# Query-key-normalised attention: streamed share for the zero matmuls, doubled instead of tripled score waves, sums of squares on TensorE, norm steps on GpSimd

## The chip, the cores and the metric

One Trainium2 chip, one of its cores. The metric is the device time of one execution in microseconds (us). Before the change it is 632.83 us, the median of three runs (632.67 to 633.11). The profiled execution is a run of its own: 633.45 us, of which the instructions span 631.5 us.

## What is computed

32 heads, 2048 queries and keys, 20 numbers per head:

```
qn = q / (sqrt((q * q).sum(-1, keepdims=True)) + 1e-6)
kn = k / (sqrt((k * k).sum(-1, keepdims=True)) + 1e-6)
logits = einsum('bhqd,bhkd->bhqk', qn, kn) * t[None, :, None, None]
out = einsum('bhqk,bhkd->bhqd', softmax(logits), v)      # B=1 H=32 S=2048 Dh=20
```

The inputs are bf16, and so is the output.

## The kernel before

**Tiles.** Four heads form a head group (`hg`, 8 of them), 512 queries a query group (4 per head group). A *tile* is 128 keys of one head against 512 queries; there are 32 x 16 x 4 = 2048. One head group and one query group make a *sub-block* (`sb`): 64 tiles, whose results add up in one PSUM bank, `psO`. There are 32 sub-blocks, and at the end of each `psO` is drained by a VectorE transpose into `accT` (L360), while TensorE may not write it.

**Two ways to exponentials.** TensorE writes a tile's scores into PSUM (L692: the four heads sit in four 32-row strips of the array, and strips run side by side). Then either ScalarE takes `exp` of two tiles at once, `psA` to `pA` (L885; here called a *wave*; `psA` holds two waves, so the scores of wave w wait until the `exp` of wave w-2 has ended), or VectorE turns a tile in `psD` into the bits of an f16 with one multiply-add to int16 (`dI`, "P1", L325), of which two shifted copies `dS` are made by adding integers: on VectorE (L340) or on GpSimd (L338). Then TensorE multiplies with `vaug` (V and a column of ones, for the denominators), L714: one matmul for a ScalarE tile, four for a VectorE tile (`dI` with `vaug` and with `vhalf`, and each `dS` with `vaug`), in four 32-column strips side by side.

**Zeros.** A matmul of zeros adds nothing to `psO` and keeps TensorE streaming (L558, 128 columns each; at the start 11 of 512 columns, L562). While `psO` drains there can be none; there the score matmuls of a wave are issued three times over (`mms * 3`), to the same place with the same result.

**Preparation.** For each head group k, q and v are loaded (L395, L405), squared (`sq`, L260) and reduced (L263) on VectorE, turned into reciprocal norms by eight small steps on VectorE (`rs0` to `rs5`, `eps`, `inv`, L282 to L289), multiplied into `kpad` and `qpad` (L304, GpSimd), and transposed by DMA into `kT` and `qT` (L414). The first head group goes in two parts: rows 0 to 3 by TensorE, and of rows 4 to 15 the `kT` rows 8 to 15 and the `qT` rows 4 to 15 by DMA.

**What sets the order.** No scheduler on the chip: `make_plan` walks a model of the core in steps of 5 ns, with costs in constants, and writes down one order for each engine; the chip then runs these orders with semaphore waits. So each engine and the DMA queue of SyncE issue strictly in order: an instruction that waits holds all behind it. The constants decide the order, not the duration of anything. `in_use` says how busy TensorE was in a window `HEATW`, and zeros are put in below `HEAT`. VectorE and GpSimd share a port: `lock` keeps VectorE's fast modes off it while GpSimd runs. Two plans are built, and a branch early in the program takes the first if no `t` is above a bound, as here.

Of the kernel before, what the change touches and what calls it, by code (L numbers as in the profile page):

```python
# [6 lines left out]
BF16 = mybir.dt.bfloat16  # L7
# [20 lines left out]
NH = 4  # L28
WAVES = (2, 2)
DBANKS = 3  # L30
NPA = 20
RING = 24
RUN_MAX = 4
# [3 lines left out]
D_LAST = 18  # L37
D_WAIT = 36
# [3 lines left out]
PREP1 = (.25,.35)  # L42
# [3 lines left out]
HOLD = 0  # L46
# [7 lines left out]
POOL_MAX = 3  # L54
ALONE = (.2, 0)
PMIN = 5
PGAP = 0.3
PVHOLD = (.22,.22)
HEAT0 = 11
HEATN = 128  # L60
HEAT = .57
HEATW = 3.41
# [3 lines left out]
ACT0 = .05  # L66
ACT1 = .24
# [10 lines left out]
PSLACK = 0.15  # L78
# [3 lines left out]
SOON = 8  # L82
DURG = 1
LOAD1 = 0.2
DJOIN = 0.3
# [60 lines left out]
def bass_standalone__qk_norm__prompt_kernel(  # L146
# [15 lines left out]
    with ExitStack() as es:  # L162
# [16 lines left out]
        vaug = [sbuf(f"vaug{i}", [128, NH, R, 32], BF16) for i in range(2)]  # L179
        vpart = {c: [sbuf(f"v{n}{i}", [128, NH, R, 32], BF16) for i in range(2)] for c, n in ((.5, "half"),)}  # L180
# [7 lines left out]
        idn = sbuf("idn", [128, 128], BF16)  # L188
        nr0 = sbuf("nr0", [128, 2, NH, 4], F32)
# [41 lines left out]
        def prep_ops(hg, r0, r1, a0=0, a1=2, pool=False):  # L231
# [9 lines left out]
            for c0 in range(r0, r1, sqn * 2 // na):  # L241
# [30 lines left out]
            def add(nm, emit, reads, writes, rate=R1, fix=0.0):  # L272
                ops.append(dve(nm, n, rate, emit, reads, writes, fix))
# [5 lines left out]
            else:  # L279

                y = ri.bitcast(F32)
                add("rs0", lambda e: e.tensor_scalar(ri, s_.bitcast(I32), -0.5, RS_MAGIC, ALU.mult, ALU.add), [SS], [K("ri")], R2)  # L282
                add("rs1", lambda e: e.tensor_tensor(rb, s_, y, ALU.mult), [K("ri"), SS], [K("rb")])
# [58 lines left out]
        def part_op(hg, c):  # L342
            b = hg % 2
            f = lambda tl: tl[b][:, :, :, :].rearrange("p h r d -> p (h r d)")
            return dve("vh", NH * R * 32, R4, lambda e: e.tensor_single_scalar(f(vpart[c]), f(vaug), c, ALU.mult),
# [34 lines left out]
        def load_qk(hg, a, part=None):  # L380
            b = hg % 2
            r0, r1 = (0, R) if part is None else PARTS[part]
            if a == 0 and hg == HG - 1:

                ops = []
                for x in range(4):
# [10 lines left out]
                        0.5, 4.0 if part != 0 else 2.2)]  # L397
# [10 lines left out]
        def tr_op(hg, which, r0, r1):  # L408
# [6 lines left out]
                       [(which + "pad", b, r) for r in range(r0, r1)], keys, 0.58 + 0.17 * (r1 - r0), 1.75 + 0.17 * (r1 - r0))  # L415
# [21 lines left out]
        def make_plan(share):  # L437
# [61 lines left out]
            def zeros(i, after=()):  # L499
                z = lambda ap_, val, key: Op("POOL", "z", lambda e: e.memset(ap_, val), after, [(key, i)], 0.5, 0.6)  # L500
                return [z(kpad[i][:, :, :, D:32], 0.0, "kz"), z(qpad[i][:, :, :, D:32], 0.0, "qz"),
                        z(vaug[i][:, :, :, D:D + 1], 1.0, "vz"), z(vaug[i][:, :, :, D + 1:32], 0.0, "vz")]
# [3 lines left out]
                               [], ["iot"], 0.5, 0.6)] + zeros(0))  # L506
# [54 lines left out]
            o = Op("PE", "heat", None, ["zt"], [("psA", 0)])  # L561
            o.info = [(lambda e, i=i: e.matmul(psA[:, (i % 3) * QW:(i % 3 + 1) * QW], zt[:, 0:128], zt[:, :])) for i in range(HEAT0)]  # L562
# [3 lines left out]
            used_w = [(0.0, 0.0, 0.0)]  # L566
# [52 lines left out]
            if share:  # L619
                for c in vpart:  # L620
                    o = part_op(0, c)
                    o.reads.append(("qpad", 0, R - 1))
                    want_dve(o, 3)
            loaded = 1
# [42 lines left out]
            def pe_put(op, mode, strips):  # L667
# [11 lines left out]
                if st - used_w[0][0] > 20:  # L679
                    del used_w[0:20]  # L680
# [651 lines left out]
```

## Time and profile before

| | |
|---|---|
| median of 3 runs | 632.83 us |
| profiled execution, its span | 633.45 us, 631.5 us |
| busy: TensorE, VectorE, ScalarE, GpSimd | 614.5, 614.1, 618.8, 445.5 us |
| `exp` instructions on ScalarE | 667 (1333 tiles) |
| tiles on VectorE | 715 |
| TensorE clock granted, mean | 0.995 |

In a line of the profile stand the source line, the engine, the operation, what is written and read, the shapes and the count; then busy time and the mean duration of one, then the idle time just before and what ended it. In a timeline the first number is the start and the second the length of a run of like instructions, in us. Consecutive instructions of an engine overlap a little in the records, so the step from one to the next is shorter than the duration of one.

### The profile page before, as it was taken

The numbers are of one execution on the slowest core, as the hardware profiler recorded it, in microseconds if no ns is written. First come the engines' busy times: TensorE is split into PE (matmuls) and PEld (weight loads), VectorE is DVE, ScalarE is ACT, GpSimd is POOL, SyncE is SP. The second block draws the span as 40 slices with busy tenths as digits, with TensorE's granted clock in tenths as the row PEclk, the third lists the DMA queues.
The fourth block names the chain that finished last, engine by engine and source line by source line (L and its number), as shares of the span: only waits on it lengthen the run. The fifth ranks groups of instructions, "written<-read, shape, count | busy, mean of one in ns | idle before, by whom it ended". The sixth has DMA issues, their size and how long they took to land.

```text
span 631.5 us, 15864 instructions
## 1 busy us (share of the span) xinstructions
PE 614.5 (97%) x6794; PEld 180.3 (29%) x6794; DVE 614.1 (97%) x869; ACT 618.8 (98%) x675; POOL 445.5 (71%) x491
## 2 busy tenths in 40 slices
PE   8999999999999999999999999999999999999996
PEld 4432222322222232223223222232222332222221
DVE  6999999999999999999999999999999999999995
ACT  6999999999999999999999999999999999999995
POOL 4586667766677776876768666776777777666772
PEclk8999999999999999999999999999999999999999
DMA  6610404041040130306031050400404022010000
GB/s 73 88 10 16 95 1 43 2 62 48 2 43 2 35 76 5 39 2 111 1 29 16 1 110 3 40 4 3 93 3 57 2 33 37 1 23 6 6 5 13
DMA packets 113772, 19.57 MB, mean 31 GB/s; under 512 B 102944, under 2 KB 113696, under 8 KB 113696
## 3 DMA queue, kind: packets, MB, share of 16 engines
q1 hardware_dynamic: 112896, 18.37, 19.9%
q8 instruction: 55, 0.90, 0.6%
q10 hardware_dynamic: 800, 0.12, 0.1%
q14 instruction: 21, 0.17, 0.1%
HBM read 7.87 MB, written 2.62 MB: 17 GB/s over the span
## 4 chain that ended last, share of the span: by engine, by line
ACT 72%; PE 26%; DVE 1%; DMA 0%; issue 0%; POOL 0%
ACT pA L885 72%; PE psO L714 12%; PE psA L692 10%; PE psD L692 2%; PE psO L558 2%; DMA qk<-in_q_dram 0%; DVE ssum L263 0%; POOL kpad L304 0%; DVE accT L360 0%; PE psD L570 0%; DVE sqs L260 0%; DVE ost L368 0%; DVE qT L585 0%; DVE rn L289 0%; DVE rec L364 0%
## 5 line engine op out<-in xcount | busy, mean ns | idle before, releaser
L885 ACT ACTIVATE pA<-psA 128x1024 f16<-128x1024 f32 (+1 forms) x667 | 614.5, 1111 | 2.0 <-PE psA L692 1.6
L338 POOL TENSOR_TENSOR dS<-dI,shc 128x256 int32<-128x256 int32 (+2 forms) x378 | 373.0, 1007 | 130.0 <-DVE dS L340 93.2
L325 DVE TENSOR_SCALAR dI<-psD 128x1024 int16<-128x1024 f32 (+1 forms) x486 | 434.1, 927 | 4.4 <-PE psD L692 1.8
L692 PE MATMUL psA<-qT,kT 32*128 32x512 bf16 x1553 | 283.0, 384 | 8.9 <-ACT pA L885 6.0
L714 PE MATMUL psO<-pA,vaug 128*32 128x512 f16 (+1 forms) x1333 | 233.7, 384 | 0.0
L714 PE MATMUL psO<-dS,vaug 128*32 128x512 f16 x1430 | 224.5, 385 | 0.0
L692 PE MATMUL psD<-qT,kT 32*128 32x512 bf16 x715 | 193.9, 383 | 0.0
L714 PE MATMUL psO<-dI,vaug 128*32 128x512 f16 x715 | 155.3, 386 | 0.0
L714 PE MATMUL psO<-dI,vhalf 128*32 128x512 f16 x715 | 152.0, 384 | 0.0
L692 PEld LDWEIGHTS psA<-qT,kT 32*128 32x128 bf16 x1553 | 69.0, 91 | 239.4 <-ACT pA L885 224.1
L340 DVE TENSOR_SCALAR dS<-dI 128x2048 int16<-128x2048 int16 (+2 forms) x182 | 122.5, 679 | 0.0
L714 PEld LDWEIGHTS psO<-dS,vaug 128*32 128x32 bf16 x1430 | 51.1, 94 | 73.2 <-issue 58.7
L714 PEld LDWEIGHTS psO<-pA,vaug 128*32 128x32 bf16 x1333 | 52.5, 94 | 37.5 <-issue 31.8
L692 PEld LDWEIGHTS psD<-qT,kT 32*128 32x128 bf16 x715 | 45.4, 91 | 22.1 <-DVE dI L325 10.2
L714 PEld LDWEIGHTS psO<-dI,vaug 128*32 128x32 bf16 x715 | 36.7, 93 | 24.5 <-issue 17.4
L714 PEld LDWEIGHTS psO<-dI,vhalf 128*32 128x32 bf16 x715 | 36.4, 94 | 22.0 <-issue 19.2
L366 POOL TENSOR_TENSOR ost<-accT,rec 128x320 bf16<-128x320 f32 x31 | 23.3, 753 | 16.7 <-DVE dS L340 9.5
L304 POOL TENSOR_TENSOR qpad<-qk,rn 128x320 bf16<-128x320 bf16 x31 | 22.0, 728 | 17.3 <-DVE dS L340 10.4
L558 PE MATMUL psO<-zt 128*128 128x128 bf16 x310 | 32.3, 228 | 0.1
L304 POOL TENSOR_TENSOR kpad<-qk,rn 128x320 bf16<-128x320 bf16 x31 | 22.2, 738 | 10.8 <-DVE dS L340 6.1
L558 PEld LDWEIGHTS psO<-zt 128*128 128x128 bf16 x310 | 19.7, 101 | 21.0 <-issue 20.1
L360 DVE STREAM_TRANSPOSE accT<-psO 128x512 f32<-128x512 f32 x32 | 22.6, 705 | 2.7 <-PE psO L714 2.7
(51 smaller groups left out, 100.1 us busy)
## 6 DMA issues: line engine op xcount, KB each, us to landing
vaug<-in_v_dram SPq DMA_DIRECT2D x32, 80.0 KB, 4.0
qk<-in_k_dram SPq DMA_DIRECT2D x7, 320.0 KB, 4.0
out_dram<-ost SPq DMA_DIRECT2D x28, 80.0 KB, 1.9
qk<-in_q_dram SPq DMA_DIRECT2D x6, 320.0 KB, 3.9
qk<-in_q_dram SPq DMA_DIRECT2D x4, 80.0 KB, 3.1
out_dram<-ost SPq DMA_DIRECT2D x7, 40.0 KB, 2.0
qk<-in_k_dram SPq DMA_DIRECT2D x1, 240.0 KB, 3.6
qk<-in_q_dram SPq DMA_DIRECT2D x1, 240.0 KB, 4.2
```

What stands on the lines that cost most here:

```text
L304: emit = lambda e, o=dst, x=src, s=sc: e.tensor_tensor(o, x, s, ALU.mult)
L325: lambda e: e.tensor_scalar(dst, psD[:, pb * QW:(pb + n) * QW], 1024.0 * LOG2E, 15360.0 - 1024.0 * LOG2K + SHIFTS[0], ALU.mult, ALU.add),
L338: lambda e: e.tensor_tensor(o.bitcast(I32), x.bitcast(I32), c, ALU.add), rd + ["shc"], wr)
L340: lambda e: e.tensor_single_scalar(o, x, float(SHIFTS[i] - SHIFTS[0]), ALU.add), rd, wr)
L360: dve("drain", QW, R1, lambda e: e.transpose(aT[:, :, :].rearrange("p b d -> p (b d)"), psO[:, :]), ["psO"], [("accT", b)], 0.03),
L366: pool_op("omul", 320, True, lambda e: e.tensor_tensor(dst, num, rcb, ALU.mult), [("accT", b), ("rec", b)], [("ost", ob, qg)]) if pool else
L558: return lambda e: e.matmul(bank, zt[:, 0:128], zt[:, 0:n], start=False, stop=False, skip_group_check=True)
L692: return lambda e: e.matmul(dst, lhsT, rhs, tile_position=(32 * hh, 0))
L714: return lambda e: e.matmul(dst, lhsT, rhs, start=first, stop=last, skip_group_check=True, tile_position=(0, 32 * hh))
L885: a = Op("ACT", "exp", lambda e, s=src, d=dst: e.activation(d, s, ACT.Exp), [("psA", slot)], [("pA", pslot, i) for i in range(WAVES[slot]) ...
```

## The change

- The planner's measure for zeros becomes the share of the last 1.7 us in which anything streamed through TensorE (before: 3.41 us, weighted by the share of strips in use).
- While `psO` drains, a wave's scores are issued twice, not three times, and below a share of 0.8.
- For head groups 1 to 7 the squares (still VectorE) are transposed by DMA (`sqT`) and summed by TensorE against a matrix of ones and zeros (`ind`): 20 matmuls of 128 columns, in five lots of four, into a `psD` bank lent for it. `rs0` and `rs1` read the sums there. `ind` is made at the start (GpSimd and VectorE).
- `rs2`, `rs3`, `rs4` and `eps` of these groups go to GpSimd.
- `vaug` and `vhalf` have 22 columns per head, not 32.
- The planner's constants change: 18 wave slots in `pA` instead of 20, at most 30 shifts waiting instead of 36, shifts of up to 6 tiles at once on VectorE and of at most 2 on GpSimd (before 4 and 3), other lead times, other latencies for loads and transposes. `LOAD1 = 0` (before 0.2): the loads of head group 1 are asked for as soon as the first scores are issued.
- The tiles come out as 719 on VectorE and 1329 on ScalarE (664 `exp` of two tiles and one of one; before 666 and one).

The built programs, instruction by instruction (all 8 head groups, the branch that runs):

```
                                     before   after
exp of two tiles + of one, ScalarE   666 + 1  664 + 1
scores into psA, TensorE             1553     1461
zeros of 128 columns, TensorE        310      137
sums of squares, TensorE             0        140
P1 of 2 tiles, of 1 tile, VectorE    229, 257 197, 325
shifts, VectorE: of 1,2,3,4,5,6 tiles 0,8,9,165,0,0  25,20,60,13,19,65
shifts, GpSimd: of 1,2,3 tiles       142,123,113  234,211,0
reduces of 1280, VectorE             14       0
DMA transposes of squares            0        14
```

SyncE's order at the start: before, k, q and v of group 0, the branch, `kT` and `qT` of group 0, then k, q and four v of group 1; after, k, q and v of group 0, k and q of group 1, the branch, four v of group 1, then `kT` and `qT` of group 0, then the transposes of the squares.

The core of the diff:

```diff
-RUN_MAX = 4
+RUN_MAX = 6
-HEAT = .57
-HEATW = 3.41
+HEAT = 0.66
+HEATQ = 0.8
+TWICE = 2
+HEATW = 1.7
-LOAD1 = 0.2
+LOAD1 = 0
+NORM_POOL = ('rs2', 'rs3', 'rs4', 'eps')
...
+            for a in (1, 0) if hg else ():
+                sq, x3 = sqs[a][:, :], qk[b][:, a, :, :, :].rearrange("p h r d -> p (h r d)")
...
+                ops.append(dma("Ts", lambda e, o=dst, x=sq: e.dma_start_transpose(o, x), keys[:1], [("sqT", a)],
+                               0.58 + 0.17 * n_, TRL + 0.17 * n_))
...
-                ops.append(dve(nm, n, rate, emit, reads, writes, fix))
+                ops.append(pool_op(nm, n, rate != R2, emit, reads, writes) if pool and nm in NORM_POOL else
+                           dve(nm, n, rate, emit, reads, writes, fix))
...
+            def step_sums():
+                o = sums_todo[0]
+                for a in range(2):
+                    t_ = P.last_w[("sqT", a)]
+                    if t_.done is None or t_.done + SEML > now:
+                        return False
+                if "at" not in o:
+                    pb = next_bank()
+                    if not empty(pb):
+                        return False
+                    o["at"] = pb
+                    lent[0] += 1
+                    on_loan[:] = [o]
+                gj = o["left"].pop(0)
+                dst = psD[:, o["at"] * QW:o["at"] * QW + 128]
+                mms = [lambda e, g=g, j=j: e.matmul(dst, sqT[:, (5 * g + j) * 128:(5 * g + j + 1) * 128],
+                                                    ind[:, j, 96 - 32 * g:224 - 32 * g], start=g + j == 0, stop=g + j == 7,
+                                                    skip_group_check=True) for g, j in gj]
...
             def in_use():
                 t0 = now - HEATW
-                return sum(max(0.0, min(b, now) - max(a, t0)) * c for a, b, c in used_w) / HEATW
+                x, u = t0, 0.0
+                for a, b in sorted(used_w):
+                    a, b = max(a, x), min(b, now)
+                    if b > a:
+                        u, x = u + b - a, b
+                return u / HEATW
...
-                        if cur > 0 and not cur_free() and in_use() < HEAT:
-                            mms, st_ = mms * 3, st_ * 3
+                        if cur > 0 and not cur_free() and in_use() < HEATQ:
+                            mms, st_ = mms * TWICE, st_ * TWICE
...
+                if sums_todo and not 0 < wait < NSWAIT and step_sums():
+                    return True
...
-                fits = lambda c: not busy or now + c <= end + PSLACK
+                st = max(now, on[-2].done + SEML + PLAG) if busy and len(on) > 1 else now
+                fits = lambda c: not busy or st + c <= end + PSLACK
```

More of the change, by code (lines that the diff above doesn't have):

```diff
@@ L45 @@
 DFIRST = 1
-HOLD = 0
+HOLD = 0.2
 DT = 0.005
@@ L66 @@
 ACT0 = .05
+LOAD0 = 2.75
+TRL = 2.25
+TRK = 1.2
+PLAG = .03
+LOCKL = 0.12
 ACT1 = .24
@@ L949, in step_qkd @@
                     return False
[L950 to L953 removed]
+                pb = next_bank()
                 if not empty(pb):
```

134 lines of the change are left out of this document (93 added, 41 removed).

## The prediction

> **What bounds the kernel now.** I read the page first: its span, the engines' busy times, and among the costliest groups that of the `exp`.
>
> ```profile
> span 631.5 us, 15864 instructions
> ...
> PE 614.5 (97%) x6794; PEld 180.3 (29%) x6794; DVE 614.1 (97%) x869; ACT 618.8 (98%) x675; POOL 445.5 (71%) x491
> ...
> L885 ACT ACTIVATE pA<-psA 128x1024 f16<-128x1024 f32 (+1 forms) x667 | 614.5, 1111 | 2.0 <-PE psA L692 1.6
> ```
>
> Three engines look full, but only one can be shown to be so: 667 `exp` leave 2.0 us of idle time. TensorE's share is padded with zeros, and VectorE has waits in it. So I asked the timeline of ScalarE for the first `exp`, the third, a stretch within one sub-block, and the last.
>
> ```profile
> 8.39 1.02 ACT L885 ACTIVATE pA<-psA 128x1024 bf16<-128x1024 f32 x1 [0.32 <-PE psA L692]
> 11.41 1.02 ACT L885 ACTIVATE pA<-psA 128x1024 f16<-128x1024 f32 x1 [1.08 <-PE psA L692]
> 311.19 13.85 ACT L885 ACTIVATE pA<-psA 128x1024 f16<-128x1024 f32 x15
> 622.94 1.64 ACT L885 ACTIVATE pA<-psA 128x1024 f16<-128x1024 f32 x2
> ```
>
> Fifteen `exp` in 13.85 us, the last of them 1.02: a step of (13.85 - 1.02)/14 = 0.9165 us. The first ends at 9.41, the last at 624.58: 615.2 us for 666 steps, the last of which is half a wave. 665 steps of 0.9165 and one of 0.5 make 610.0. So ScalarE loses only 5.2 us between its first and its last `exp`, and 1.2 of these stand in the head: the second ends near 10.33, the third at 12.43, which is 2.10 for a step. The remaining 4.0 us have to be found, and they lie where `psO` drains:
>
> ```profile
> 308.49 1.30 PE L692 MATMUL psA<-qT,kT 32*128 32x512 bf16 x8
> 309.42 0.38 PE L692 MATMUL psD<-qT,kT 32*128 32x512 bf16 x1
> 309.63 0.59 PE L692 MATMUL psA<-qT,kT 32*128 32x512 bf16 x4
> ```
> ```profile
> 308.15 1.20 ACT L885 ACTIVATE pA<-psA 128x1024 f16<-128x1024 f32 x1
> ```
> ```profile
> 309.35 1.02 ACT L885 ACTIVATE pA<-psA 128x1024 f16<-128x1024 f32 x1
> ```
> ```profile
> L360 DVE STREAM_TRANSPOSE accT<-psO 128x512 f32<-128x512 f32 x32 | 22.6, 705 | 2.7 <-PE psO L714 2.7
> ```
>
> The `exp` of 309.35 ends at 310.37, that before it at 309.35: a step of 1.02, 0.105 too long. Its scores are a tripled wave: six of the eight matmuls from 308.49. They run in two strips, three in each one after another; a second pair adds 0.21 (0.59 less 0.38 in the third row). So the last pair starts at 308.93 and, 0.38 long, ends at 309.31. ScalarE should have begun at 309.24, as each of the fifteen begins 1.02 - 0.9165 = 0.105 before its forerunner ends. There are 32 drains, 31 of them before the last `exp`; 4.0/31 = 0.13 a drain. I went through ScalarE's steps one by one: 31 steps but the head's are more than 0.1 too long, and each is at the first tripled wave of a drain.
>
> **The change part by part.** The sum is made against the profiled 631.5 us; the profiled run took 633.45, the median of the runs is 632.83, so a difference of spans is taken off the median.
>
> (1) Two `exp` less (667 to 665): 2 x 0.9165 = -1.8. VectorE gets four tiles more, and has to have the room:
>
> ```profile
> L325 DVE TENSOR_SCALAR dI<-psD 128x1024 int16<-128x1024 f32 x229 | 277.2, 1211 | 2.6 <-PE psD L692 1.3 <-PE psA L692 0.5
> ...
> L325 DVE TENSOR_SCALAR dI<-psD 128x512 int16<-128x512 f32 x257 | 171.7, 674 | 1.8 <-PE psO L558 0.8 <-PE psD L692 0.5
> L338 POOL TENSOR_TENSOR dS<-dI,shc 128x768 int32<-128x768 int32 x113 | 165.2, 1466 | 70.8 <-DVE dS L340 45.6 <-DVE sqs L260 9.7 <-DVE rsb L283 2.5
> ...
> L338 POOL TENSOR_TENSOR dS<-dI,shc 128x512 int32<-128x512 int32 x123 | 127.7, 1039 | 47.9 <-DVE dS L340 39.5 <-DVE vhalf L345 2.4 <-DVE sqs L260 1.8
> L340 DVE TENSOR_SCALAR dS<-dI 128x2048 int16<-128x2048 int16 x165 | 114.3, 697 | 0.0
> L338 POOL TENSOR_TENSOR dS<-dI,shc 128x256 int32<-128x256 int32 x142 | 85.7, 612 | 11.3 <-DVE dS L340 8.1 <-DVE ssum L286 1.2 <-DVE ssum L285 1.0
> ...
> L263 DVE TENSOR_REDUCE ssum<-sqs 128x64 f32<-128x1280 bf16 x14 | 20.6, 1474 | 0.0
> ...
> L340 DVE TENSOR_SCALAR dS<-dI 128x1024 int16<-128x1024 int16 x8 | 3.4, 428 | 0.0
> ...
> L315 POOL TENSOR_TENSOR rn<-rn,tb 128x64 f32<-128x64 f32 x7 | 2.3, 330 | 0.0
> ...
> L286 DVE TENSOR_TENSOR ssum<-ssum,rsa 128x128 f32<-128x128 f32 x7 | 2.0, 291 | 0.0
> ```
>
> The reduces go (-20.6); four steps of about 0.25 to 0.29 in seven groups go to GpSimd (-7); P1 costs 277.2 x 197/229 + 171.7 x 325/257 = 455.6 instead of 448.9 (+7). A shift takes, from 697 for 2048 and 428 for 1024, about 0.16 + 0.135 per tile; with the new lengths (202 instructions, 782 tiles, before 182 and 703) that is 138 against 124 (+14). VectorE ends some 7 us lighter by these rows. GpSimd's shifts: 234 x 0.612 + 211 x 1.039 = 362 instead of 379; the 28 norm steps take between 0.2 (VectorE's own price) and 0.6 (its 256-element sum) each; I take 0.4, by the 0.33 of the 64-element product: +11. So neither engine becomes the bound; GpSimd stays under 450 of 631. If the cover were gone, a tile late on VectorE would hold the next scores on TensorE's queue, and through them an `exp`.
>
> (2) The third repeat goes: 0.21 less per tripled wave, twice the 0.105 that it was late. The plain drains lose all of their excess; the few that were later than 0.21 keep some hundredths. -3.8 (bounds: 0, if the excess has another cause, and -4.0).
>
> (3) Zeros 310 to 137: they stand in gaps of TensorE, hidden by the `exp`. Cost 0 as long as the clock holds (a rival, below). In the head they are not free:
>
> ```profile
> 7.83 0.53 PE L692 MATMUL psA<-qT,kT 32*128 32x512 bf16 x4 [0.57 <-DVE qT L585]
> 8.30 2.53 PE L558 MATMUL psO<-zt 128*128 128x128 bf16 x22
> 10.76 0.61 PE L692 MATMUL psA<-qT,kT 32*128 32x512 bf16 x2
> ```
> ```profile
> 7.97:11.38 3.41, 3.41 (x30) 2.45 (x26) 3.13 (x11) 2.04 (x3) 1.33 (x3) 0.50 0.85 50
> 11.38:620.00 608.62, 600.18 (x6672) 174.10 (x6672) 601.46 (x835) 607.98 (x660) 438.05 (x476) 1.00 0.20 30
> ```
>
> 22 zeros took 2.5 us because the granted clock was 0.50 from 7.97 to 11.38 (the column after the counts), and the third wave's scores stood behind them. The new order has 18 there: four times 0.115, -0.4, or all of the 1.2 if that half-clock stretch does not come.
>
> (4) The start of SyncE's queue. `kT` rows 8 to 15 of group 0 leave when `kpad` is ready, at 13.69; the first scores that read them stand at 19.94 in `psD`, in the thirteenth wave, and in the changed order at the same wave. But now six loads are issued ahead of that transpose:
>
> ```profile
> 2.83 6.07 SPq L405 DMA_DIRECT2D vaug<-in_v_dram  x4
> 13.69 1.37 SPq L414 DMA_TRANSPOSE kT<-kpad  x1
> 22.21 1.44 SPq L414 DMA_TRANSPOSE qT<-qpad  x1
> 23.69 0.90 SPq L395 DMA_DIRECT2D qk<-in_k_dram  x1
> 24.64 0.52 SPq L395 DMA_DIRECT2D qk<-in_q_dram  x1
> 25.20 6.68 SPq L405 DMA_DIRECT2D vaug<-in_v_dram  x4
> ```
> ```profile
> vaug<-in_v_dram SPq DMA_DIRECT2D x32, 80.0 KB, 4.0
> ...
> kT<-kpad SPq DMA_TRANSPOSE x8, 4.9
> ```
> ```profile
> DMA to landing us min/median/max: 3.7/4.3/6.0
> ```
> ```profile
> L1276 SPq TENSOR_LOAD <-tmx x1: 719/719/719, 8.9 to 8.9; - x1
> ```
> ```profile
> 19.94 0.39 PE L692 MATMUL psD<-qT,kT 32*128 32x512 bf16 x2
> ...
> 20.73 0.39 PE L692 MATMUL psA<-qT,kT 32*128 32x512 bf16 x2
> ```
>
> SyncE is done with group 0's v at 8.90. Issuing group 1's k, q and v took 31.88 - 23.69 = 8.2 us; so it reaches the transpose at 17.1, or at about 18 if the branch in between, of which one instruction takes 0.72, does not overlap with the queue's draining. From issue to landing the transposes took 3.7 to 6.0 us (third fence), `kT` 4.9: it lands at 22.4 (20.8 to 24.0). TensorE then stands at those `psD` scores, with everything behind them: 0.79 to the next wave's scores (19.94 to 20.73), 0.42 until its `exp`, 1.02 for that. This `exp`, the fourteenth, ends 2.3 us after the landing, at 24.7; now it ends at 22.5 (12.43 + 11 x 0.9165). So the head costs +2.2 (bounds: +0.6 and +3.8; -0.4 to -1.2 if the loads do not hold the queue). What (3) gains in the head is swallowed by it. Nothing later is late: `qT` is ready only at 22.2.
>
> (5) The sums of squares add a wait: lots of four matmuls behind two more DMA transposes, with the next wave's scores behind them on TensorE. The matmuls (20 x 7, each 0.115 or less like a zero) lie in TensorE's gaps: the scores must start only 0.42 before the `exp`, so about 0.4 of each 0.9165 is spare. The wait costs 0 if the order has left 4 us after each pair, and at most 6.0 - 4.0 - 0.4 = 1.6 in each of 7 groups, if the slowest transpose came each time. I take +0.5 for this, the norm chain's longer way over GpSimd (its end, `kT` of the next group, has tens of us in hand) and the smaller `pA`. The tail after the last `exp` keeps its 7 us.
>
> Sum: -1.8 - 3.8 + 2.2 + 0.5 = -2.9: 632.83 - 2.9 = 629.9 us.
>
> **The rivals.**
>
> (a) The loads do not hold the transpose back: the head gains 0.8 (between 0.4 and 1.2) instead of losing 2.2, and nothing new waits. -1.8 - 3.8 - 0.8 = -6.4: 626.4. For it: k and q alone were issued in 1.4 us. Against: both series of four v above took over 6.
>
> (b) The transpose waits behind the v data, too: it starts only when the last v has landed, 4.0 after an issue that began some 1.7 before SyncE is free, so 2.3 later: head +4.5, 632.2. The Trainium skill (DMA: Bandwidth & Descriptors, section Queues, rings and completion order) says that each DMA engine consumes descriptors in ring order. In the runs shown every transpose was issued into an empty queue, so the trace does not decide it.
>
> (c) The wait at the sums, on the other side: each of the 7 groups stands for 1.0 us at the lots: +7 instead of +0.5, 636.4. It decides from (2.9 + 0.5)/7 = 0.5 us per group on. For it: the `kT` transposes spread from about 4 to 6. Against: 0.4 of slack in each wave, and two transposes are short ones (10 blocks, not 16).
>
> (d) The clock falls to 0.50 in some drains. The head's stretch cost ScalarE 1.2 us; at that price three eat the gain of (1) to (5), and eleven, one drain in three, give 643. For it: the head's stretch, and 173 zeros less. Against: 1.00 throughout 608 us; and counted in the two orders, with 0.21 for 512 columns, four successive waves stream for at least 0.58 of their time after the change, and 0.54 before it. The Trainium skill (TensorE: Matmul & The Clock Gate, Part 1) has a free-running window of about 3.4 us, and half clock after an idle one; the head's 3.41 us agree with the window, and by that rule a drain with doubled scores is not idle.
>
> (e) The third repeat was not what held the `exp`: (2) gives 0, so 633.7. Against: 31 of 31.
>
> **How the numbers follow.** Forecast 0.46, (a) 0.24, (b) 0.09, (c) 0.10, (d) 0.08, (e) 0.03. 0.2% of the time is 1.27 us, about what a measurement of this kernel can tell from no change. Faster (under 631.56): (a), nine tenths of the forecast, a little of (b): 0.70. Same: most of (b), the rest of the forecast, (e): 0.12. Slower: (c), (d): 0.18. Range 626.2 to 633.5: from (a) to the forecast with a head at its upper bound and two more us; the forecast alone 628 to 631.6.
>
> **What would show it.** At each drain the first doubled wave's `exp` has a step of 0.92, not 1.02: (2) right. 665 `exp`: (1). SyncE's transpose of `kT` starts after 17, and the fourteenth `exp` comes with 1 to 3 us of idle time before it, released by the `psD` scores: (4); without it, (a). The lots of sums with idle time before them on a DMA: (c). PEclk under 1.00 after 20 us: (d). The prediction is wrong if ScalarE's idle time between 30 and 620 us is more than 2 us, or if its step within a sub-block is not 0.9165.

## The result, and the profile after

The changed kernel takes 628.96 us in the median of 20 runs (628.04 to 634.42), the kernel before 632.67 us in 20 runs beside them (631.93 to 634.34): a ratio of 0.9949, with a 95% interval of 0.9937 to 0.9962. That is 3.7 us. The profiled run of the change took 629.45 us, its span is 627.6, 3.9 less than before. All ranges here show every run; some runs have stretches at half the TensorE clock, and the ratios leave out those that are disturbed most.

From the page of the changed kernel: the span, the engines, and the groups of `exp`, of P1, and of the shifts on GpSimd.

```profile
span 627.6 us, 15789 instructions
...
PE 606.2 (97%) x6686; PEld 165.9 (26%) x6686; DVE 610.3 (97%) x885; ACT 614.2 (98%) x673; POOL 443.1 (71%) x588
...
L971 ACT ACTIVATE pA<-psA 128x1024 f16<-128x1024 f32 (+1 forms) x665 | 609.9, 1164 | 1.3 <-PE psA L772 1.1
L371 POOL TENSOR_TENSOR dS<-dI,shc 128x512 int32<-128x512 int32 (+1 forms) x445 | 358.6, 813 | 126.2 <-DVE dS L373 91.5
L358 DVE TENSOR_SCALAR dI<-psD 128x512 int16<-128x512 f32 (+1 forms) x522 | 436.8, 875 | 3.1 <-PE psD L772 2.2
```

The bound is still ScalarE: 665 `exp` with 1.3 us of idle time. (The mean of 1164 ns says nothing of its speed: an `exp` that begins earlier, beside its forerunner, is longer in the records. Only the step from one end to the next counts.) The page also has the chain that ended last, by engine: before, ScalarE 72% and TensorE 26%; after, as here:

```profile
ACT 92%; PE 6%; DVE 1%; DMA 0%; issue 0%; POOL 0%; SPq 0%
```

The 26% are not lost time: the drains lost 4.0 us, 0.6% of the span. Where an `exp` starts late because of TensorE, the chain passes over to TensorE's own work. (e1 and e2 below take away and put back the third copy alone: there the chain has ACT 94% and PE 3%, and ACT 61% and PE 34%.) Here is one drain of the changed kernel, in the timeline: first the doubled wave on TensorE, then the `exp` that runs beside it and the one that reads it.

```profile
305.77 0.60 PE L772 MATMUL psA<-qT,kT 32*128 32x512 bf16 x4
```
```profile
305.51 1.13 ACT L971 ACTIVATE pA<-psA 128x1024 f16<-128x1024 f32 x1
```
```profile
306.42 1.13 ACT L971 ACTIVATE pA<-psA 128x1024 f16<-128x1024 f32 x1
```

The doubled wave is four matmuls, two in each strip, and ends at 306.37. The `exp` that reads it starts at 306.42 and ends at 307.55; the one before ended at 306.64. A step of 0.91, where the same place before the change had 1.02.

The whole span can be put together for both kernels. With steps of 0.9165 us (and a last one of 0.49 for the half wave), what is left over between the first and the last `exp` is lost time; behind the last `exp` comes the tail.

| us | before | after | difference |
|---|---|---|---|
| end of the first `exp` | 9.41 | 10.06 | +0.65 |
| full steps | 665 x 0.9165 = 609.47 | 663 x 0.9165 = 607.64 | -1.83 |
| lost between first and last | 5.20 | 1.67 | -3.53 |
| end of the last `exp` | 624.58 | 619.85 | -4.73 |
| tail | 6.97 | 7.78 | +0.81 |
| span | 631.5 | 627.6 | -3.9 |

Of the 1.67 us lost after the change, 0.75 stand in the half-clock stretch of the head, 0.39 in three steps at 24.6, 26.6 and 28.6 us, and 0.53 in the other 590 us, where before the drains lost 4.0.

The largest of these later steps is at the sums of squares. TensorE, then ScalarE, at that place:

```profile
265.69 0.84 PE L730 MATMUL psD<-ind,sqT 128*128 128x128 bf16 x12
266.47 0.60 PE L772 MATMUL psA<-qT,kT 32*128 32x512 bf16 x4
```
```profile
267.11 1.02 ACT L971 ACTIVATE pA<-psA 128x1024 f16<-128x1024 f32 x1
```

Three lots of sums, twelve matmuls, run in one go ahead of a doubled wave, which so ends at 267.07; its `exp` is 0.24 late. No lot of sums in this run waits for a DMA transpose.

Now the start, on VectorE: first before the change, then after it.

```profile
3.97 0.82 DVE L263 TENSOR_REDUCE ssum<-sqs 128x32 f32<-128x640 bf16 x1
4.70 0.18 DVE L530 TENSOR_REDUCE tmx<-tb 128x1 f32<-128x32 bf16 x1
5.08 0.18 DVE L278 TENSOR_SCALAR rsa<-nr 128x32 f32<-128x32 f32 x1 [0.20 <-ACT nr L277]
```
```profile
4.24 0.19 DVE L566 TENSOR_REDUCE tmx<-tb 128x1 f32<-128x32 bf16 x1 [0.30 <-DMA tb<-in_t_dram]
4.34 0.81 DVE L293 TENSOR_REDUCE ssum<-sqs 128x32 f32<-128x640 bf16 x1
5.07 0.31 DVE L662 SCALAR_TENSOR_TENSOR iof<-iof 128x160 f32<-128x160 f32 x1
5.42 0.32 DVE L663 TENSOR_SCALAR ind<-iof 128x160 bf16<-128x160 f32 x1
5.65 0.17 DVE L309 TENSOR_SCALAR rsa<-nr 128x32 f32<-128x32 f32 x1
```

The maximum over `t` was behind the first reduce and is now ahead of it, where it waits for the load of `t`; and the two steps that make `ind` stand between the reduce and `rsa`. So `rsa`, on which `kpad`, the first transposes and the first scores depend, starts 0.57 later (5.08 to 5.65). The first scores start 0.56 later (7.83 to 8.39), and the first `exp` ends 0.65 later. The difference is the clock: after the change the first scores fall wholly into the half-clock stretch, which begins at 8.3, and take 0.61 instead of 0.53. In e2 below, which has the same order on VectorE but no such stretch there, they take 0.40 (the change, then e2):

```profile
8.39 0.61 PE L772 MATMUL psA<-qT,kT 32*128 32x512 bf16 x4 [0.57 <-DVE qT L621]
```
```profile
8.35 0.40 PE L772 MATMUL psA<-qT,kT 32*128 32x512 bf16 x4 [0.56 <-DVE qT L621]
```

SyncE's queue and the scores behind it, after the change:

```profile
8.87 1.17 SPq L428 DMA_DIRECT2D qk<-in_k_dram  x1
10.09 0.59 SPq L428 DMA_DIRECT2D qk<-in_q_dram  x1
11.67 4.96 SPq L438 DMA_DIRECT2D vaug<-in_v_dram  x4
16.68 2.86 SPq L447 DMA_TRANSPOSE kT<-kpad  x1
```
```profile
DMA to landing us min/median/max: 4.7/4.7/4.7
```
```profile
20.06 0.39 PE L772 MATMUL psD<-qT,kT 32*128 32x512 bf16 x2
...
21.90 0.38 PE L772 MATMUL psD<-qT,kT 32*128 32x512 bf16 x1 [0.25 <-DVE dI L358]
21.90 0.39 PE L772 MATMUL psA<-qT,kT 32*128 32x512 bf16 x2
```

(The second fence is the view of the tile `kT`, up to 24 us.) The transpose does leave 3.0 us later than before (13.69), and lands at 21.4. But the `psD` scores of the thirteenth wave, at 20.06, run without a wait. They read keys that are there already; those of 21.90 are the first that need rows 8 and up, and in this run the rows have landed 0.5 us before.

### The profile page after: what moved, and what is told of

The parts are those of the page before. It is cut to its first block, busy times and chain, and to the rows that moved or that the text cites. A ratio compares the mean times of both kernels' runs of the same rounds, so it can differ in the third digit from the quotient of the medians.

```text
span 627.6 us, 15789 instructions
## 1 busy us (share of the span) xinstructions
PE 606.2 (97%) x6686; PEld 165.9 (26%) x6686; DVE 610.3 (97%) x885; ACT 614.2 (98%) x673; POOL 443.1 (71%) x588
## 4 chain that ended last, share of the span: by engine, by line
ACT 92%; PE 6%; DVE 1%; DMA 0%; issue 0%; POOL 0%; SPq 0%
ACT pA L971 92%; PE psO L794 2%; PE psA L772 2%; PE psO L594 1%; DMA tb<-in_t_dram 0%; PE psD L772 0%; DVE dI L358 0%; PE psD L730 0%; POOL kpad L337 0%; DVE accT L393 0%; PE psD L606 0%; DVE ost L401 0%; SPq L428 0%; DVE qT L621 0%; DVE rn L322 0%
## 5 line engine op out<-in xcount | busy, mean ns | idle before, releaser
L971 ACT ACTIVATE pA<-psA 128x1024 f16<-128x1024 f32 (+1 forms) x665 | 609.9, 1164 | 1.3 <-PE psA L772 1.1
L371 POOL TENSOR_TENSOR dS<-dI,shc 128x512 int32<-128x512 int32 (+1 forms) x445 | 358.6, 813 | 126.2 <-DVE dS L373 91.5
L358 DVE TENSOR_SCALAR dI<-psD 128x512 int16<-128x512 f32 (+1 forms) x522 | 436.8, 875 | 3.1 <-PE psD L772 2.2
L794 PE MATMUL psO<-pA,vaug 128*22 128x512 f16 (+1 forms) x1329 | 245.6, 383 | 0.0
L794 PE MATMUL psO<-dS,vaug 128*22 128x512 f16 x1438 | 232.5, 383 | 0.2
L794 PE MATMUL psO<-dI,vaug 128*22 128x512 f16 x719 | 161.2, 383 | 0.2
L794 PE MATMUL psO<-dI,vhalf 128*22 128x512 f16 x719 | 157.3, 382 | 0.2 <-DVE dS L373 0.2
L373 DVE TENSOR_SCALAR dS<-dI 128x3072 int16<-128x3072 int16 (+5 forms) x202 | 140.7, 708 | 0.0
L794 PEld LDWEIGHTS psO<-dS,vaug 128*22 128x22 bf16 x1438 | 49.6, 89 | 72.7 <-issue 60.5
L794 PEld LDWEIGHTS psO<-pA,vaug 128*22 128x22 bf16 x1329 | 51.3, 89 | 35.3 <-issue 29.1
L794 PEld LDWEIGHTS psO<-dI,vaug 128*22 128x22 bf16 x719 | 35.4, 89 | 28.5 <-issue 18.1
L794 PEld LDWEIGHTS psO<-dI,vhalf 128*22 128x22 bf16 x719 | 35.2, 89 | 20.8 <-issue 18.2
L337 POOL TENSOR_TENSOR qpad<-qk,rn 128x320 bf16<-128x320 bf16 x31 | 22.0, 727 | 13.7 <-DVE dS L373 7.0
```

Source lines behind the costliest of these rows:

```text
L337: emit = lambda e, o=dst, x=src, s=sc: e.tensor_tensor(o, x, s, ALU.mult)
L358: lambda e: e.tensor_scalar(dst, psD[:, pb * QW:(pb + n) * QW], 1024.0 * LOG2E, 15360.0 - 1024.0 * LOG2K + SHIFTS[0], ALU.mult, ALU.add),
L371: lambda e: e.tensor_tensor(o.bitcast(I32), x.bitcast(I32), c, ALU.add), rd + ["shc"], wr)
L373: lambda e: e.tensor_single_scalar(o, x, float(SHIFTS[i] - SHIFTS[0]), ALU.add), rd, wr)
L794: return lambda e: e.matmul(dst, lhsT, rhs, start=first, stop=last, skip_group_check=True, tile_position=(0, 32 * hh))
L971: a = Op("ACT", "exp", lambda e, s=src, d=dst: e.activation(d, s, ACT.Exp), [("psA", slot)], [("pA", pslot, i) for i in range(WAVES[slot]) ...
```

## The experiments

Every kernel was run beside the kernel before on the same chip. The kernel before took 633.21 us beside e1 to e4, 632.81 beside e5 to e8 and 633.27 beside e9 to e12, and 632.67 beside the change; so times of different groups are compared only to about half a microsecond. Each ratio is to the kernel before. In e1 and e2 only repeated matmuls with the same result are left out or added.

**e1. The old order without the third copy.** The order of before the change stays as it is; only the third pair of matmuls is not issued.

```diff
 # before the change, where a tripled wave has been placed
+                        op.info = op.info[:2 * len(us)]
```

> The kernel before with its own order on every engine, only that the third copy of the scores is left out where a wave was tripled (110 matmuls less; same 667 exp, same zeros). Theory, the third copy ends 0.1 us too late at each of 31 drains: 3.3 to 4.0 us less than before, 628.7 to 629.4, and steps of 0.92 at the drains. Rival, the exp at a drain waits for something else: within 0.5 us of before, 632.2 to 633.2, and steps of 1.02 stay. Rival, without the third copy the clock falls in the drains: granted clock under 0.99, and more than 633.

630.11 us (629.17 to 630.53), a ratio of 0.9948 (0.9935 to 0.9961): all that the change brings. It is 3.1 us less than the kernel before, a little under the 3.3 to 4.0 of the theory. With 667 `exp` the last ends at 620.00, and 0.67 us are lost instead of 5.20. Of these 4.5 us, 3.5 are the drains. The other 1.0 is the half-clock stretch of the head, which did not come in the profiled run (granted clock 0.999; in the other three runs 0.995 to 0.996). A drain of this kernel, the `exp` of the doubled wave (306.50) and its forerunner:

```profile
305.51 1.20 ACT L886 ACTIVATE pA<-psA 128x1024 f16<-128x1024 f32 x1
```
```profile
306.50 1.13 ACT L886 ACTIVATE pA<-psA 128x1024 f16<-128x1024 f32 x1
```

They end at 306.71 and 307.63: a step of 0.92. The third copy was what made the drains late, and everything else in the change adds up to nothing that the intervals can tell.

**e2. The third copy put back into the new order.**

```diff
 # after the change, where a doubled wave has been placed
+                        if len(mms) > len(us):
+                            op.info = mms + mms[:len(us)]
```

> The kernel after with its own order, only that each doubled wave is issued a third time (132 matmuls more). Theory: the steps of 1.02 come back at 31 drains, 3.0 to 4.0 us more than after: 632.0 to 633.0. Rival, the gain of after does not hang on the copies: 628.5 to 629.5.

635.74 us (633.17 to 640.67), a ratio of 1.0047 (1.0017 to 1.0077). Behind 33 us 38 steps that are 0.1 or more too long are back, and 4.78 us are lost there, where the change lost 0.53. That is the effect of the third copy. The rest is not: in the head 0.69 is lost at a late `kT` (see below e8), and 2.4 in a half-clock stretch that begins at 24.2. Such a drain, TensorE and ScalarE:

```profile
309.84 0.82 PE L772 MATMUL psA<-qT,kT 32*128 32x512 bf16 x6
```
```profile
309.68 1.02 ACT L973 ACTIVATE pA<-psA 128x1024 f16<-128x1024 f32 x1
```
```profile
310.70 1.02 ACT L973 ACTIVATE pA<-psA 128x1024 f16<-128x1024 f32 x1
```

Six matmuls, ending at 310.66, and the `exp` after them at 310.70, just when its forerunner ends: a step of 1.02. The effect of the one line is shown in both directions.

**e3. The loads of group 1 late again.**

```diff
-LOAD1 = 0
+LOAD1 = 0.2
```

> The kernel after with the loads of head group 1 asked for at a progress of 0.2, as before (same 665 exp and 719 VectorE tiles). The prediction's step 4 (six loads hold back the transpose of kT, which holds the scores): 1 to 2.2 us less than after, 626.8 to 628.0. Rival, read from the trace of after (the transpose lands at 21.4, the scores that read it stand at 21.9): within 0.6 us of after, 628.4 to 629.6, with the transpose issued near 14.3 and the same steps of the exp around it.

632.47 us (627.86 to 633.38), a ratio of 0.9969 (0.9944 to 0.9994). The transpose of `kT` is back ahead of the six loads:

```profile
14.24 1.37 SPq L447 DMA_TRANSPOSE kT<-kpad  x1
```

It leaves 2.4 us earlier than in the profiled run of the change and lands at 17.4, and no scores wait for it. The best run, 627.86, is 0.2 below the best of the change (628.04), which is less than the chips differ. The median, 632.47, is above what the theory and the rival said, and the clock goes with it: the four slowest of the six runs have a granted clock of 0.984 to 0.988, the other two 0.995 and 0.998. In the profiled run five half-clock windows follow one another from 9.1 to 26.2 us, and the steps in them are 6.0 us too long; outside them 0.6 are lost. So this run gives no saving that can be measured, and it does not tell the price of the loads' place: that needs the profiles of the other variants, below e8.

**e4. The sums on VectorE again** (no transposes of squares, no sums on TensorE; the rest as after the change).

```diff
-            for a in (1, 0) if hg else ():
+            for a in ():
...
-            for c0 in range(r0, r1, sqn * 2 // na) if not hg else ():
+            for c0 in range(r0, r1, sqn * 2 // na):
```

> The kernel after with the sums of squares back on VectorE as reduces (no transposes of squares, no sums on TensorE); the planner then ends at 709 VectorE tiles and 670 exp. Theory, the sums on TensorE cost nothing and are worth the 5 exp: 5 x 0.9165 = 4.6 us more than after, 633.5, no slower than that in its steps. Rival, the waits at the sums eat part of it: 630 to 632.

640.4 us (637.28 to 649.69), a ratio of 1.0107 (1.0073 to 1.014), well above the 633.5 of the theory. The reduces take VectorE's time, so the order has 670 `exp` and 709 tiles on VectorE: five `exp` more are 4.6 us. The tail is 9.5 us, 1.9 are lost outside half-clock stretches, and 7.2 inside one of 17.1 us that begins at 13.9. In the new order the sums on TensorE are worth at least the 4.6 us of five `exp`; how much of the rest belongs to them, this run does not separate.

**e5 and e6. More zeros in the head; and in e6 the first norms ahead of `ind` as well.**

```diff
 # e5 and e6
-                if in_use() >= HEAT or cur == NSB or not cur_free():
+                if in_use() >= (HEAT if now > 35 else 0.9) or cur == NSB or not cur_free():
 # e6 alone
-LOAD0 = 2.75
+LOAD0 = 2.2
```

In e6, moreover, the first step of `ind` has to wait for the first `qpad`, and both are due at 0.8 us instead of 4.

> The kernel after with zeros asked for up to a share of 0.9 in the first 35 us (elsewhere 0.66 as in after); 665 exp, 718 VectorE tiles. Theory, the half-clock windows of the head (one in most executions of after, five or six in the slow ones) come from too little streaming between 8 and 30 us: at most one such window in the profile, no run above 630.5, median 628 to 629 beside a before of 632.7. Rival, the windows come by chance of their phase whatever streams: runs above 632 as before, granted clock of 0.983 to 0.989 in some.

> As the run with head zeros, and the three VectorE steps that after put into the first chain (the maximum of t ahead of the first reduce, and the two steps that make the matrix of ones and zeros behind it) go back behind it; 666 exp. Theory: the first exp ends 0.6 us earlier than in after, 9.4 instead of 10.06, and the time is 0.6 less for it and 0.9 more for the one exp: within 0.5 of the run with head zeros alone. Rival: the first exp waits for a load, not for these steps, and ends at 10.0 again.

e5: 630.52 us (630.30 to 631.07), ratio 0.9964 (0.9952 to 0.9977), 187 zeros. There is no half-clock stretch in its head, but two waves are 0.5 late each, both behind a transfer: the first result matmuls wait 0.51 for v data, and at 22.17 scores wait for `kT`. One half-clock stretch came at 518.8 and cost 1.1. The theory's 628 to 629 is missed. e6: 630.56 us (629.84 to 632.79), ratio 0.9966 (0.9953 to 0.998), 666 `exp`. Its first `exp` ends at 9.33, 0.73 sooner than after the change. The order on VectorE is 0.51 of this (the first scores start at 7.88 instead of 8.39); the rest is that these scores run at the full clock. But the earlier start only runs into the transfers sooner: 0.84 is lost at 13.8 behind a wait of 0.75 for v data, and scores wait 1.13 for `kT` up to 22.15, where a half-clock stretch follows. The wait and the stretch together lose 3.0. Neither beats the change.

**e7. The norm steps on VectorE again.**

```diff
-NORM_POOL = ('rs2', 'rs3', 'rs4', 'eps')
+NORM_POOL = ()
```

> The kernel after with all norm steps of head groups 1 to 7 on VectorE again; 666 exp, 716 VectorE tiles. Theory, the move is worth what the planner makes of it: one exp, 0.9 us more than after, 629.9. Rival, GpSimd's steps hold VectorE at the shared port, so that undoing the move costs nothing or gains: 628 to 629.

632.15 us (630.36 to 636.59), ratio 0.9993 (0.9973 to 1.0013), where the theory said 629.9. 716 tiles on VectorE and 666 `exp`: one step of 0.92. Another 1.9 of the profiled run are lost where `kT` comes late and the clock falls after it. The best run is 2.3 above the best of the change, so there is more to it, and what it is stays open.

**e8. Zeros only in the first 35 us.**

```diff
-                if in_use() >= HEAT or cur == NSB or not cur_free():
+                if in_use() >= (HEAT if now < 35 else 0.0) or cur == NSB or not cur_free():
```

> The kernel after with zeros only in the first 35 us (94 of 137 are left; 665 exp, 718 VectorE tiles). The prediction's rival (d), zeros hold the clock: half-clock windows around the drains after 35 us, each costing some 1 us, time over 633. The other reading, the scores and products alone keep the clock: PEclk 1.00 from 35 us on, time as after, 628.5 to 629.5.

636.42 us (634.00 to 641.21), ratio 1.0056 (1.0035 to 1.0077), with 93 zeros and the same 665 `exp`. The windows view around the first of its two half-clock stretches, in pieces of 3.41 us ahead of it, and then the stretch:

```profile
144.57:147.98 3.41, 3.41 (x44) 0.81 (x36) 3.41 (x5) 3.41 (x4) 2.42 (x4) 1.00 0.02 5
147.98:151.40 3.42, 2.54 (x26) 0.82 (x22) 3.42 (x5) 3.42 (x5) 2.62 (x4) 0.99 0.00 0
```
```profile
151.40:165.05 13.65, 13.40 (x85) 2.34 (x84) 9.84 (x13) 9.88 (x11) 7.69 (x9) 0.50 0.00 1
```

Where TensorE ran 26 matmuls in 3.42 us instead of 44, and was idle for 0.88 of them, the clock fell. Two of the `exp` in the stretch:

```profile
153.27 1.02 ACT L971 ACTIVATE pA<-psA 128x1024 f16<-128x1024 f32 x1 [0.48 <-PE psA L772]
154.77 1.02 ACT L971 ACTIVATE pA<-psA 128x1024 f16<-128x1024 f32 x1 [0.48 <-PE psD L772]
```

A step is then 1.50, not 0.92. Both stretches, 13.7 and 10.2 us or seven windows of 3.41, lost 8.8 us: 1.26 a window. The zeros after 35 us do hold the clock, and the 44 that the change leaves there were enough in its profiled run.

**The late `kT` in e2 and e5 to e9.** These kernels issue the six loads ahead of the transpose as the change does. In their profiled runs SyncE gets to it at 17.9 to 18.4 us, where the profiled run of the change had 16.68: issuing the four v took them 5.8 to 6.3 us, and it 4.96. They also had no half clock between 8 and 12 us. Their first `exp` ends 0.2 to 0.7 sooner, and the 0.75 that the stretch then cost the change is not lost. So TensorE comes to the scores that need rows 8 and up at 20.8 to 21.2, before the rows have landed (21.8 to 22.6). In the profiled run of the change it ran them at 21.90, with the rows there since 21.4. The timelines of e8, then of e7:

```profile
22.77 0.37 PE L772 MATMUL psD<-qT,kT 32*128 32x512 bf16 x1 [1.87 <-DMA kT<-kpad]
```
```profile
22.39 0.37 PE L772 MATMUL psD<-qT,kT 32*128 32x512 bf16 x1 [1.40 <-DMA kT<-kpad]
```

1.87 and 1.40 us of idle TensorE, and an `exp` 1.36 and 0.89 too late; in e2 it is 0.69, in e5 0.50, in e9 0.67. (In e2 and e9 the profile names `dI` as the releaser, but `kT` lands just then too: 18.04 + 3.8 = 21.8 for scores at 22.01, 17.99 + 4.0 = 22.0 for scores at 22.16.) In e10 the transpose leaves at 18.28, but the first `exp` ends at 10.07 and the head has its half-clock stretch (8.6 to 12.0), as in the change, and nothing waits. So the price of the loads' place lies between 0 and 1.4 us, and the profiled run of the change is at the lucky end: a half-clock stretch that cost it some 1.0 us hid the wait.

It has a second price. The windows view of e7, in pieces of 3.41 us that end where the half clock begins, and the first piece of it:

```profile
16.78:20.19 3.41, 3.41 (x38) 1.69 (x36) 2.30 (x11) 3.41 (x5) 0.72 (x1) 1.00 0.83 48
20.19:23.60 3.41, 2.01 (x21) 0.69 (x21) 2.59 (x4) 2.63 (x4) 2.97 (x4) 1.00 0.63 120
23.60:27.02 3.42, 3.42 (x26) 0.89 (x24) 3.42 (x5) 2.86 (x4) 1.98 (x3) 0.51 0.50 96
```

The window with the wait in it has TensorE busy for 2.01 of 3.41 us, and the clock falls behind it. Laid out from its half-clock stretches in this way, e2, e6 and e11 had 2.21, 2.28 and 2.27 us in the window ahead of the fall, and e4 1.79, where TensorE had waited 1.53 us for v data:

```profile
10.44:13.85 3.41, 1.79 (x19) 0.80 (x17) 2.10 (x8) 2.19 (x4) 1.51 (x2) 1.00 1.04 200
```

Against that, the longest wait, that of e8, is cut in two by the edge of a window, and the clock held:

```profile
18.24:21.65 3.41, 2.66 (x29) 1.10 (x26) 2.50 (x7) 3.41 (x5) 2.12 (x4) 1.00 1.01 111
21.65:25.06 3.41, 2.29 (x26) 0.88 (x26) 2.12 (x4) 2.15 (x4) 2.08 (x4) 1.00 0.62 120
```

In the 14 profiled runs, every fall between 10 and 100 us came behind a window with 1.79 to 2.28 us; of the windows in that time that held, the emptiest had 2.29 to 2.42. This is no fixed bound. In the windows that begin at 4 to 7 us, e3 fell behind 1.91 us, and e9 held behind 1.74:

```profile
5.65:9.06 3.41, 1.91 (x21) 0.94 (x20) 2.78 (x9) 2.56 (x6) 2.37 (x4) 1.00 0.88 52
```
```profile
4.03:7.44 3.41, 1.74 (x12) 0.72 (x11) 3.00 (x8) 1.74 (x4) 1.17 (x3) 1.00 0.98 142
```

So the busy time of a window is not all that decides. The edges of the windows differ from run to run, and so the same wait costs a stretch of half clock in one run and nothing in the next. Not all falls are of this kind: those of e5 at 518.8, of e10 at 271.4 and the second of e8 came behind windows with 2.8 to 3.1 us, and the first of e8 behind 2.54; the change held the clock behind two windows of 2.78 (at 284.8 and 530.5).

**e9, e10, e11. The measure of before in the new order:** everywhere (e9), in the first 35 us (e10), and there with the first norms ahead of `ind` (e11).

```diff
+            def in_use0():
+                t0 = now - 3.41
+                return sum(max(0.0, min(b, now) - max(a, t0)) for a, b in used_w) * .25 / 3.41
...
 # e9, and the same for the doubled waves; e10 and e11: if now < 35
-                if in_use() >= HEAT or cur == NSB or not cur_free():
+                if in_use0() >= .57 or cur == NSB or not cur_free():
```

> After the change, but zeros and doubled waves are again decided by the measure of before (share of 3.41 us, weighted by strips, below 0.57): 665 exp, as after the change, and 199 zeros instead of 137. Theory (the new measure costs nothing by itself, but leaves the half-clock windows to chance): 628.0 to 629.5 in the median, and no run above 631, where three of 20 runs of the change had 632 to 634. Rival (the half-clock windows come whatever the measure): the same median, with the late runs as often as before. Rival (the zeros cost time as such): above 630.

> After the change, with the measure of before for zeros in the first 35 us alone: 666 exp. Theory: one exp more than the change, +0.9, so 629 to 630, and no run above 631.5, since the half-clock windows of the late runs lie in the head. Rival (they also lie in the drains, where the new measure stays): late runs remain, and their half-clock windows then stand after 35 us.

> As the one before, and the first exp as early as before the change (the two ind steps and the step on t behind the first norms): 666 exp, first exp ending at 9.35 instead of 10.06. Theory: 0.7 less than the one before, 628.3 to 629.3, if nothing later in the head takes it back. Rival (the head is limited by later steps, the tiles of VectorE near 24 us): no gain, 629 to 630.

e9: 631.18 us (631.13 to 631.34), ratio 0.997 (0.9958 to 0.9982), 198 zeros. The theory said 629.5 at most. The number is the one that the last rival gave, but its cause isn't: the last `exp` ends at 619.86, as after the change (619.85), so the 61 zeros more cost ScalarE nothing that shows. (Its head has no half-clock stretch, but the late `kT`.) The tail is 9.39 us instead of 7.78. The end of the chain of waits shows it, for the change and then for e9 (columns: start, length, engine, what it wrote, how many):

```profile
618.94 2.29 PE psO L794 x37
621.25 0.73 DVE accT L393
```
```profile
618.53 4.45 PE psO L794 x76
623.00 0.73 DVE accT L393
```

The planner left 76 matmuls for the end instead of 37, so the last drain starts 1.75 later.

e10: 632.46 us (630.21 to 638.76), ratio 1.0004 (0.9979 to 1.0029). e11: 635.86 us (631.62 to 647.37), ratio 1.0038 (1.0009 to 1.0067). Here both theories fall: eight of e10's twelve runs took more than 632 us, and the gain of the earlier first `exp` in e11 (9.31) is not to be seen. The measure in the head does not explain e10's late runs. Up to 40 us e9 and e10 have the same order on every engine and on SyncE, and none of e9's six runs took more than 631.4. That speaks for the order behind 40 us, where e10 has the new measure, as its rival had it; the one half-clock stretch of its profiled run behind the head, at 271.4, fits. It is not shown: one run of each is profiled, and neither is a late one. Zeros are put in by the planner's model, and a transfer that is late on the chip is not in it: in e11 TensorE waits 1.04 us for v data, up to 12.15, and the half clock begins at 13.5. In its profiled run, the slowest of the twelve, the half clock held up to 61.3 us. Against the change itself, six runs of e9 without a late one decide nothing, since the change had three in 20.

**e12. Two copies in the planner of before**, so that it makes its own order for them.

```diff
-                            mms, st_ = mms * 3, st_ * 3
+                            mms, st_ = mms * 2, st_ * 2
```

> Before the change, with two copies instead of three in the planner itself, so that its order changes too: 669 exp, 710 tiles on VectorE, 338 zeros. Theory (the third copy is the whole gain of 3.1 us; each exp more costs a step of 0.92): 633.2 - 3.6 + 1.8 = 631.4. Rival (the number of exp does not count, since the last tiles are bounded by something else): 630.1, as with the third copy left out of the old order.

633.83 us (632.65 to 646.46), ratio 1.0008 (0.9999 to 1.0018), where the theory said 631.4: nothing is left of the gain. (The run of 646.46 has a granted clock of 0.998, so it is not the clock that made it late; what did is not known.) The same two copies as in e1, and 0.87 us lost between first and last `exp`; but the planner now gives 669 `exp`, and the last ends at 622.50, 2.5 later than in e1, of which two steps are 1.83. The tail is 8.75 instead of 7.36, with 65 matmuls at its end:

```profile
621.13 4.44 PE psO L714 x65
625.59 0.73 DVE accT L360
```

An `exp` more does cost a step; and the tail is a term of its own, which the number of `exp` does not tell.

## Why the prediction was right or wrong

The time, 628.96, lies 0.9 below the forecast of 629.9, within the forecast's own range. That it came so close is in part luck: the head cost 1.6 us less than forecast, the tail 0.8 more.

(1) Two `exp` less: -1.83, as predicted, and e12 shows the price of a step. Neither VectorE nor GpSimd became the bound. VectorE's busy time fell by 3.8 us where the rows had given 7, and GpSimd's by 2.4 where they had given 6.

(2) The third copy: -3.8 predicted. Lost time outside the head went from 4.0 to 0.53, of which at least 0.24 belong to (5); behind 33 us e1 alone took it from 4.0 to 0.47, and e2 brought it from 0.53 to 4.78. This step is shown by undoing it and by doing it alone. Rival (e) is out.

(3) The head's zeros: 18 instead of 22 in the half-clock stretch; the third step went from 2.10 to 1.67, 0.43 less for the 0.4 predicted. That stretch came at 8.3 again, so the bound of 1.2 was not reached.

(4) is the step that failed. "TensorE then stands at those `psD` scores, with everything behind them" was priced at +2.2, and in the profiled run of the change nothing stands. The first half of the step was right: reached "at 17.1, or at about 18", landing "at 22.4 (20.8 to 24.0)"; measured 16.68 and 21.4 in the change, 17.9 to 18.4 and 21.8 to 22.6 in the variants with this queue. The mechanism is right too, as e7 and e8 show. The place was wrong: "the first scores that read them stand at 19.94 in `psD`". The row was taken for the reader without looking at which keys it reads. The first three tiles in `psD` ran at 19.2 to 20.5 in e2 and e5 to e9, before the rows landed; the fourth is the first that waits. It ran at 21.38 before the change; in the new order TensorE comes to it between 20.8 and 22.1. That takes the wait from 2.2 down to between 0 and 1.4. So one half of rival (a) came in the profiled run, that nothing new waits, but not by its reason: the loads do hold the queue. Its other half, a head that gains 0.8, did not come.

The head lost 0.65 by another way that the prediction did not see: the order on VectorE ahead of `rsa`. The late start and the half-clock stretch together hid the transpose in that run: e2, e5, e8 and e9 have the same order on VectorE there but no such stretch, and meet the wait. Three steps at 24 to 29 us, where VectorE's tiles begin, added 0.39. With (3) that makes about +0.6 for the head, not +2.2: the largest error of the sum.

(5) was taken at +0.5. At the sums 0.24 was lost in one place, by twelve matmuls in a row and not by a DMA, so rival (c) did not come. "The tail after the last `exp` keeps its 7 us" was wrong by 0.8: of the last output the page has 4.0 us from issue to landing where it had 2.4 before, in one run each, so that this is not shown to belong to the change. What e9 and e12 do show is that the order moves the tail by more than that.

Rival (b), the transpose behind the v data, is out: it lands 3.8 to 4.7 us after its issue, where it took 4.8 before.

Rival (d), the clock, was judged rightly for the median run, and its price of 1.2 for a stretch of one window holds (1.26 in e8). Its argument against, that a drain with doubled scores is not idle, does not hold up: in e8 the clock fell behind windows in which TensorE was busy for 2.5 and 3.1 us. But it is the rival that matters: three of the 20 runs took 632.57, 634.21 and 634.42 us, at a mean granted clock of 0.989 and 0.983 where the others have 0.994 to 0.999. (634.42 - 628.5)/1.2 is about five windows, and the clock agrees: 0.015 x 632.5 / 0.5 = 19 us at half clock. The prediction asked whether the drains would trigger it and took the head's one stretch as fixed. The variants have theirs mostly between 9 and 31 us. In e2, e6 and e7 they follow the wait for `kT`, so there (d) is a consequence of (4). In e4 and e11 they follow a wait for v data of group 0, which are loaded ahead of the six loads as before the change, and that of e3 begins ahead of both waits. That the three late runs of the change itself had such a stretch is argued from their clocks; no profile shows one of them.

## What to carry to other kernels

When a change has many parts, issue the old order with one part left out: here a single repeated matmul pair was worth the whole gain, and in the profiled run the remaining parts cancelled (two `exp` less against a later first `exp`, sums ahead of a wave, and a tail). Before a late transfer is priced, look up which instruction first reads the part that comes late, not the first that reads the tile; and count with it the clock, which can fall behind the wait. A planner's order is one thing: each change of a constant moves the number of `exp`, the head and the tail together, so a variant is read by these three terms and not by its time alone.

## What the hardware did that was not expected

The half-clock stretches that end before the kernel does are whole numbers of one window: 3.41, 6.8, 10.2, 13.7 and 17.1 us, and 47.8 in e11, and each begins on one grid in a run (the two of e8, at 151.4 and 421.0, are 79 windows apart). Full work does not end a stretch at once: in e4 the clock stayed at half for five windows in which TensorE was busy all the time by its records.

```profile
13.90:31.00 17.10, 17.10 (x117) 6.45 (x114) 9.99 (x21) 12.92 (x13) 5.25 (x8) 0.50 0.53 60
```

What brings the full clock back, after one window in e7's case and five in e4's, was not found. The Trainium skill (TensorE: Matmul & The Clock Gate, Part 1) has a free-running window of 3413 ns, and the grid agrees with it. It also has the full clock come back after one busy window, and the half clock after an idle one; the five windows of e4, and the falls behind windows with 1.79 to 2.28 busy us, differ from that, and here the runs decide. The kernel before the change has such runs too, though rarely: one of 643.12 us among 30 and one of 645.71 among 23, at granted clocks of 0.975 and 0.971, beside medians of 633.27 and 632.81.
